# Two feed-forward blocks after an attention: where the split weights lie, how many steps multiply with unsplit weights, and which engine converts and cuts

## The chip, the cores and the metric

One core of one Trainium2 chip runs the whole kernel. The metric is the device time in microseconds (us). TensorE is called PE here, VectorE DVE, ScalarE ACT, GpSimd POOL, and the queue that issues all DMAs SP.

## The reference

An induced attention turns x (12480 x 128) into new tokens by way of 32 inducing points; then two feed-forward blocks follow, each 128 to 2048 to 128:

```python
x = mab(x, mab(I, x))                       # softmax attention, twice
h = x @ moe_w_in;  g = h * clip(h + 3, 0, 6) / 6;   x = g @ moe_w_out
h = x @ moe2_w_in; r = maximum(h, 0);               x = (r * r) @ moe2_w_out
```

The weights arrive as 64-bit floats, and the kernel reads them as 64-bit integers and makes float32 of them itself.

## The kernel before, in words

Tokens lie along the free dimension, in 25 chunks of 512 (one of 192). A chunk takes 8 **steps** of two 128-row feature blocks in each feed-forward block, so that there are K = 200 steps of each. Loop k of the main loop (line 757) runs step k of the first block and step j = k - 11 of the second. The stages of a step are `up1` (L597, two matmuls into `h`), `gate1` (L605 on ACT, L606 on DVE, giving `g`), then `high1` (ACT L615 or POOL L617), which rounds `g` to float32r, `low1` (DVE or POOL, L625), which subtracts that from `g`, and two loops after `up1` the product with w_out, `down1`. In the second block these are `up2` (L674), `relu2` (L685) and `square2` (L689) on ACT, `high2` (ACT L699 or POOL L694), `low2` (DVE L705) and, three loops behind `up2`, `down2`. A split product (`down`, L645, and `up2`) takes three float32r matmuls per feature block: high by high, low weights by high, high by low. In the first N1 = 13 steps of the first block `down_whole` (L633) multiplies the unsplit float32 `g` with the unsplit float32 weights instead; for those steps `high1` and `low1` return at once.

The first weight, w1a (kind "a"), is mixed with the attention's result; the others come in four pieces each of 128 x 512: "b" is moe_w_out, "c" moe2_w_in, "d" moe2_w_out. A piece is loaded as 64-bit words (`load_piece`, L153 or L158), made into float32 by `convert` (DVE L174 masks the sign, POOL L178 clamps, ACT L183 scales the low word, DVE L185 and L189 shift and join, POOL L194 adds), and a b, c or d piece is later split by `cut`: a float32r high part (`wh`, L210 on POOL, L214 on ACT or L216 on DVE) and a low part (`wl`, L218 on DVE or POOL). float32 pieces of kinds b, c and d (`w32`) share 8 rotating buffers, and each high and each low part has a buffer of its own.

What sets the order: `tick()` is called at 26 places before the main loop (16 in the loop over eight groups of tokens, then around the attention's end) and twice in each loop, so that loop k holds ticks 26 + 2k and 27 + 2k. `PLAN` gives for each piece the tick of its conversion, the tick of its cut and the engines of the cut's two instructions. SP runs its DMAs in program order throughout. The other engines run in written order up to the end of the first attention (line 750); from there to loop 23 a scheduler orders each engine's instructions at build time, by written order and by its own model of when each can start; from loop KM = 24 on the written order holds again. In each engine's queue an instruction that waits holds up all behind it.

The attention of chunk c + 1 is spread over loops 8c to 8c + 3: scores on PE (L485), `att_shift` on DVE (L505 to L510), an exponential (L519), `att_norm` (L526 to L534), and `att_spread` (L571 to L581), which sends the result through 16 DMAs of SP (L581) into `a_t`, the right side of `up1` eight steps later. Three PSUM buffers `h` serve `up1`, `up2` and the scores together. At the end of a chunk's `down1`, ACT L662 and DVE L663 read `yacc`, of which there is one, into `yh` and `yl`.

Of the kernel before, what the change touches and what calls it, by code (L numbers as in the profile page):

```python
# [10 lines left out]
F32 = mybir.dt.float32  # L11
F32R = mybir.dt.float32r
# [4 lines left out]
ALU = mybir.AluOpType  # L17
# [20 lines left out]


PLAN = {  # L40
    ("a", 0): (4, None, ""),
    ("a", 1): (6, None, ""),
    ("a", 2): (8, None, ""),
    ("a", 3): (10, None, ""),
    ("b", 0): (13, 58, "sv"),
    ("b", 1): (17, 54, "sv"),
    ("b", 2): (22, 50, "vp"),
    ("b", 3): (29, 55, "vv"),
    ("c", 0): (32, 47, "sp"),
    ("c", 1): (26, 33, "sp"),  # L50
    ("c", 2): (36, 46, "pp"),
    ("c", 3): (50, 57, "sp"),
    ("d", 0): (38, 54, "sp"),
    ("d", 1): (53, 58, "sp"),
    ("d", 2): (53, 62, "pv"),
    ("d", 3): (58, 62, "pv"),
}

HIGH1_S = {0, 1, 3, 4, 6, 7, 9, 13, 14, 18, 19, 20, 22, 23}
LOW1_P = {1, 2, 4, 5, 6, 7, 8, 11}  # L60
HIGH2_P = {0, 1, 6, 7, 10, 12}
LOW2_P = {}
N1 = 13
OFF = 11
L1, L2 = 2, 3
MIX = (0, 3)
PRE = 26
KM = 24
RA, RB = 4, 4
WB = 8  # L70
TAIL = 8
LAST = 2

# [2 lines left out]
def induced_attention_then_two_ffn(  # L76
# [84 lines left out]
    whole, parts, raws, held = {}, {}, {}, []  # L161


    def float_of(item):
        kind, q = item
        if kind == "a":
            return wpool.tile([P, CW], F32, tag=f"hb{q}", name="wa")
        return cv.tile([P, CW], F32, tag="w32", name="w32", bufs=WB)

    def convert(item):  # L170
        words = raws.pop(item)
        low, high = words[:, :, 0], words[:, :, 1]
        e = cv.tile([P, CW], U32, tag="cve", name="cve")
        nc.vector.tensor_scalar(  # L174
            out=e, in0=high, scalar1=0x7FFFFFFF, scalar2=0x7FFFFFFF,
            op0=ALU.bitwise_and, op1=ALU.bitwise_and,
        )
        nc.gpsimd.tensor_scalar(  # L178
            out=e.bitcast(F32), in0=e.bitcast(F32), scalar1=MOST, scalar2=LEAST,
            op0=ALU.min, op1=ALU.max,  # L180
        )
        r = cv.tile([P, CW], I32, tag="cva", name="cva")
        nc.scalar.mul(r, low, 2.0 ** -29)  # L183
        yield
# [12 lines left out]
        while waiting and not todo and sum(i[0] != "a" for i in held) < RB:  # L197
            load_piece(waiting.pop(0))

    def cut(item):  # L200
        kind, q = item
        hi, lo = (
            (wpool if kind == "b" else wpool2).tile([P, CW], F32R, tag=f"{u}{kind}{q}", name=f"w{u}")
            for u in "hl"
        )
        w = whole[item]
        assert ("a", q) not in whole or kind != "b"
        on = [engine_of[i] for i in PLAN[item][2]]
        if on[0] is nc.gpsimd:
            nc.gpsimd.tensor_scalar(  # L210
                out=hi, in0=w, scalar1=1.0, scalar2=1.0, op0=ALU.mult, op1=ALU.mult
            )
        elif on[0] is nc.scalar:
            nc.scalar.copy(hi, w)  # L214
        else:
            nc.vector.tensor_copy(hi, w)  # L216
# [433 lines left out]
    def down1(k):  # L650
# [184 lines left out]
```

## Time and profile before

| | us |
|---|---|
| three runs: median (lowest, highest) | 989.15 (986.91, 991.25) |
| the profiled execution, its own time | 988.34 |
| its span in the trace | 986.5 |
| ACT busy in the span | 816.5 (83%) |
| POOL busy in the span | 274.1 (28%) |

The span is what the profiler sees between the first and the last instruction; 1.8 us of the execution's time lie around it. All rows below are from that one execution.

### The profile page before, as it was taken

The page shows a single profiled execution, that of the slowest core. Times are in us where ns is not written, and L with a number is a line of the kernel's source. Part 1 is how long each engine was busy: PE and PEld are TensorE (multiplying, and loading weights), DVE is VectorE, ACT ScalarE, POOL GpSimd, SP SyncE. Part 2 cuts the span into 40 slices and gives each one's busy share as a digit, 9 for nine tenths or more (in the row PEclk, how much of TensorE's full clock was granted, in tenths as well). Part 3 has the DMA queues.
Part 4 walks back from the last instruction along what each step waited for, and adds up shares of the span by engine and source line. Part 5 has one row for each costly group of instructions (what it writes and reads, how often), then busy time and mean ns, then how long its engine had stood idle before and what let it go on. Part 6 is the DMA issues. An engine that isn't in the chain of part 4 may idle for free.

```text
span 986.5 us, 12958 instructions
## 1 busy us (share of the span) xinstructions
PE 958.1 (97%) x4614; PEld 766.4 (78%) x4614; DVE 810.9 (82%) x980; ACT 816.5 (83%) x928; POOL 274.1 (28%) x417
## 2 busy tenths in 40 slices
PE   8877899999999999999999999999999999999998
PEld 6534678888888888888888888888888888888886
DVE  4788978888888888888887798888888888888864
ACT  6556878888888888888888968888888888888886
POOL 2365312222222222222221232222222222222213
PEclk9897999999999999999999999999999999999999
DMA  9522010110110110100100011001001001000000
GB/s 344 169 71 79 16 33 2 32 32 2 32 33 2 32 33 2 31 26 1 32 26 6 28 33 27 6 27 33 7 27 33 7 27 32 8 15 22 1 11 21
DMA packets 32879, 34.54 MB, mean 35 GB/s; under 512 B 7600, under 2 KB 25008, under 8 KB 32304
## 3 DMA queue, kind: packets, MB, share of 16 engines
q1 hardware_dynamic: 32816, 33.73, 10.9%
q8 instruction: 36, 0.59, 0.3%
q14 instruction: 27, 0.22, 0.1%
HBM read 21.18 MB, written 6.39 MB: 28 GB/s over the span
## 4 chain that ended last, share of the span: by engine, by line
PE 89%; DVE 6%; ACT 2%; DMA 1%; POOL 1%; issue 1%; SPq 0%; DVEq 0%; POOLq 0%
PE oacc L645 26%; PE h L674 26%; PE yacc L645 25%; PE h L597 9%; DVE g L606 1%; DMA raw<-in_w1a 1%; PE ps L485 1%; DVE cve L189 1%; DVE cve L185 1%; DMA xg<-in_xT 1%; PE yacc L633 1%; ACT g L605 1%; PE xt L336 0%; POOL cve L178 0%; POOL wl L218 0%
## 5 line engine op out<-in xcount | busy, mean ns | idle before, releaser
L606 DVE SCALAR_TENSOR_TENSOR g<-g,h 128x1024 f32<-128x1024 f32 (+1 forms) x200 | 238.4, 1193 | 112.9 <-ACT g L605 109.9
L605 ACT ACTIVATE g<-h,three 128x1024 f32<-128x1024 f32 (+1 forms) x200 | 219.1, 1096 | 116.0 <-PE h L597 115.5
L705 DVE TENSOR_TENSOR lo<-g,hi 128x1024 fp32r<-128x1024 f32 (+2 forms) x201 | 241.1, 1200 | 16.4 <-PE oacc L645 10.4
L625 DVE TENSOR_TENSOR lo<-g,hi 128x1024 fp32r<-128x1024 f32 (+1 forms) x187 | 222.3, 1189 | 2.3 <-POOL hi L617 2.3
L689 ACT ACTIVATE g<-g 128x1024 f32<-128x1024 f32 (+2 forms) x201 | 206.6, 1028 | 0.5
L685 ACT ACTIVATE g<-h 128x1024 f32<-128x1024 f32 (+2 forms) x201 | 199.7, 994 | 6.5 <-PE h L674 6.5
L617 POOL TENSOR_SCALAR hi<-g 128x1024 fp32r<-128x1024 f32 (+1 forms) x180 | 185.5, 1030 | 30.5 <-ACT g L685 16.4
L699 ACT CAST hi<-g 128x1024 fp32r<-128x1024 f32 (+2 forms) x188 | 192.1, 1023 | 0.0
L674 PE MATMUL h<-yh,wh 128*128 128x512 f32 (+1 forms) x400 | 154.4, 386 | 2.5 <-ACT g L685 1.5
L674 PE MATMUL h<-yh,wl 128*128 128x512 f32 (+1 forms) x400 | 154.2, 385 | 0.0
L674 PE MATMUL h<-yl,wh 128*128 128x512 f32 (+1 forms) x400 | 153.9, 385 | 0.0
L597 PE MATMUL h<-at,m 128*128 128x512 f32 (+1 forms) x400 | 129.2, 404 | 9.9 <-DVE st L505 5.7
L645 PE MATMUL oacc<-hi,wh 128*128 128x512 f32 (+1 forms) x400 | 122.4, 387 | 0.0
L645 PE MATMUL oacc<-hi,wl 128*128 128x512 f32 (+1 forms) x400 | 121.6, 385 | 0.0
L645 PE MATMUL oacc<-lo,wh 128*128 128x512 f32 (+1 forms) x400 | 121.5, 385 | 0.0
L645 PE MATMUL yacc<-hi,wh 128*128 128x512 f32 (+1 forms) x374 | 114.2, 387 | 3.7 <-DVE yl L663 3.7
L805 POOL COPY turn<-lo 128x1 f32<-128x1 f32 x113 | 21.6, 191 | 337.9 <-DVE lo L625 337.9
L645 PE MATMUL yacc<-lo,wh 128*128 128x512 f32 (+1 forms) x374 | 113.9, 386 | 0.0
L645 PE MATMUL yacc<-hi,wl 128*128 128x512 f32 (+1 forms) x374 | 113.9, 386 | 0.0
L597 PEld LDWEIGHTS h<-at,m 128*128 128x128 f32 x400 | 72.9, 189 | 34.0 <-issue 10.1
L674 PEld LDWEIGHTS h<-yh,wh 128*128 128x128 f32 x400 | 75.3, 188 | 19.1 <-ACT g L685 2.3
L674 PEld LDWEIGHTS h<-yl,wh 128*128 128x128 f32 x400 | 75.2, 188 | 15.3
(118 smaller groups left out, 937.1 us busy)
## 6 DMA issues: line engine op xcount, KB each, us to landing
outT<-osb SPq DMA_DIRECT2D x23, 256.0 KB, 2.2
xc<-in_xT SPq DMA_DIRECT2D x22, 256.0 KB, 2.8
xg<-in_xT SPq DMA_DIRECT2D x4, 1024.0 KB, 7.1
at<-ah SPq DMA_DIRECT2D x184, 16.0 KB, 1.8
at<-al SPq DMA_DIRECT2D x184, 16.0 KB, 1.8
raw<-in_w1a SPq DMA_DIRECT2D x4, 512.0 KB, 8.8
raw<-in_w1b SPq DMA_DIRECT2D x4, 512.0 KB, 8.8
raw<-in_w2a SPq DMA_DIRECT2D x4, 512.0 KB, 4.0
```

The lines of the kernel that those rows point to most:

```text
L597: nc.tensor.matmul(h1[k][:, u, :size[c]], lhsT=m4[:, f * P:(f + 1) * P], rhs=a_t[c], start=True, stop=True)
L605: nc.scalar.activation(g1[k], h, AF.Relu, bias=three)
L606: nc.vector.scalar_tensor_tensor(out=g1[k], in0=g1[k], scalar=6.0, in1=h, op0=ALU.min, op1=ALU.mult)
L617: nc.gpsimd.tensor_scalar(out=hi1[k], in0=g1[k], scalar1=1.0, scalar2=1.0, op0=ALU.mult, op1=ALU.mult)
L625: (nc.gpsimd if k in LOW1_P else nc.vector).tensor_tensor(out=lo1[k], in0=g1.pop(k), in1=hi1[k], op=ALU.subtract)
L645: nc.tensor.matmul(acc, lhsT=w[:, f * P:(f + 1) * P], rhs=g[:, u, :], start=(p == 0 and n == 0), stop=(p == NP - 1 and n == 5),)
L674: nc.tensor.matmul(h2[k][:, u, :size[c]], lhsT=w, rhs=y, start=(n == 0), stop=(n == 2))
L685: nc.scalar.activation(g2[k][:, u, :], h[:, u, :n], AF.Relu)
L689: nc.scalar.activation(g2[k][:, u, :], g2[k][:, u, :], AF.Square)
L699: nc.scalar.copy(hi2[k][:, u, :], g2[k][:, u, :])
L705: (nc.gpsimd if k in LOW2_P else nc.vector).tensor_tensor(out=lo2[k][:, u, :], in0=g[:, u, :], in1=hi2[k][:, u, :], op=ALU.subtract)
L805: nc.gpsimd.tensor_copy(turn[:n], behind_it)
```

## The change

Two constants grow: N1 from 13 to 16 steps with unsplit weights in the first block, and a new N2 = 8 does the same in the second block. Every clamp moves from POOL to DVE, every cut takes ACT for the high and DVE for the low part, and a conversion runs its mask, clamp, scaling, shift and join within one tick. Each float32 b, c and d piece has a buffer of its own, and the low part of a piece is written where the float32 of the piece before it lay (for b0 that of c3; c0 and d0 have an extra buffer each). Raw buffers of b, c and d grow from 4 to 7. The ticks of nearly all conversions and cuts change. The last lines of `down2` use the chunk's size for 512, which is the last chunk's size too.

```diff
+    ("a", 0): (4, None), ("a", 1): (6, None), ("a", 2): (8, None), ("a", 3): (10, None),
-    ("b", 0): (13, 58, "sv"),
-    ("b", 1): (17, 54, "sv"),
-    ("b", 2): (22, 50, "vp"),
-    ("b", 3): (29, 55, "vv"),
-    ("c", 0): (32, 47, "sp"),
-    ("c", 1): (26, 33, "sp"),
-    ("c", 2): (36, 46, "pp"),
-    ("c", 3): (50, 57, "sp"),
-    ("d", 0): (38, 54, "sp"),
-    ("d", 1): (53, 58, "sp"),
-    ("d", 2): (53, 62, "pv"),
-    ("d", 3): (58, 62, "pv"),
+    ("b", 0): (13, 53), ("b", 1): (17, 57), ("b", 2): (22, 61), ("b", 3): (26, 65),
+    ("c", 0): (33, 36), ("c", 1): (37, 40), ("c", 2): (41, 44), ("c", 3): (45, 49),
+    ("d", 0): (48, 62), ("d", 1): (52, 66), ("d", 2): (56, 70), ("d", 3): (60, 74),
...
-HIGH1_S = {0, 1, 3, 4, 6, 7, 9, 13, 14, 18, 19, 20, 22, 23}
-LOW1_P = {1, 2, 4, 5, 6, 7, 8, 11}
-HIGH2_P = {0, 1, 6, 7, 10, 12}
-N1 = 13
+HIGH1_S = {18, 19, 20, 22, 23}
+HIGH2_P = {10, 12}
+N1, N2 = 16, 8
-RA, RB = 4, 4
-WB = 8
+RA, RB = 4, 7
...
     def float_of(item):
...
-        return cv.tile([P, CW], F32, tag="w32", name="w32", bufs=WB)
+        return (wpool if kind == "b" else wpool2).tile([P, CW], F32, tag=f"w{kind}{q}", name="w32")
+
+    def lower_of(item):
+        kind, q = item
+        pool, tag = (wpool if kind == "b" else wpool2), f"w{kind}{q - 1}"
+        if q == 0:
+            pool, tag = wpool2, {"b": "wc3", "c": "lc", "d": "ld"}[kind]
+        return pool.tile([P, CW], F32R, tag=tag, name="wl")
...
     def convert(item):
...
-        nc.gpsimd.tensor_scalar(
+        nc.vector.tensor_scalar(
             out=e.bitcast(F32), in0=e.bitcast(F32), scalar1=MOST, scalar2=LEAST,
             op0=ALU.min, op1=ALU.max,
         )
         r = cv.tile([P, CW], I32, tag="cva", name="cva")
         nc.scalar.mul(r, low, 2.0 ** -29)
-        yield
         nc.vector.tensor_scalar(
...
     def cut(item):
...
-        w = whole[item]
+        w = whole.pop(item)
...
+        nc.scalar.copy(hi, w)
         yield
-        on[1].tensor_tensor(out=lo, in0=w, in1=hi, op=ALU.subtract)
+        lo = lower_of(item)
+        nc.vector.tensor_tensor(out=lo, in0=w, in1=hi, op=ALU.subtract)
...
     def high2(k):
+        if k < N2:
+            return
...
     def low2(k):
+        if k < N2:
+            return
...
     def down2(k):
...
+        if k < N2:
+            down_whole(oacc[c], g2.pop(k), "d", p)
+        else:
+            down(oacc[c], hi2.pop(k), lo2.pop(k), "d", p, by_side=k == K - 1)
```

## Rows read from the trace of the kernel before

**Rows 1.** The page's busy time and share of the span by engine.

```profile
PE 958.1 (97%) x4614; PEld 766.4 (78%) x4614; DVE 810.9 (82%) x980; ACT 816.5 (83%) x928; POOL 274.1 (28%) x417
PEclk9897999999999999999999999999999999999999
```

**Rows 2.** Windows: stretch, length, busy PE, PEld, DVE, ACT, POOL, granted clock, DMA.

```profile
45.00:72.00 27.00, 21.52 (x60) 9.35 (x60) 22.94 (x40) 16.06 (x23) 16.05 (x16) 1.00 0.24 68
72.00:85.00 13.00, 5.74 (x19) 2.51 (x19) 12.93 (x18) 6.06 (x9) 7.09 (x6) 0.67 0.45 144
85.00:128.60 43.60, 38.29 (x144) 26.64 (x143) 37.37 (x46) 32.68 (x35) 18.00 (x16) 0.94 0.05 13
128.60:300.00 171.40, 171.40 (x779) 140.37 (x778) 144.90 (x160) 148.80 (x157) 41.70 (x67) 1.00 0.08 24
```

**Rows 3.** Chain in order of time: start, us, what; one whole step, two split ones.

```profile
50.08 1.72 PE yacc L633 x4
...
129.22 1.36 PE h L674 x6
...
133.76 1.36 PE h L674 x6
```

**Rows 4.** PE's timeline at loops 0, 8, 10 and 19, and one wait.

```profile
45.10 0.74 PE L597 MATMUL h<-at,m 128*128 128x512 f32 x2 [0.68 <-DVE cve L174]
...
73.75 0.70 PE L597 MATMUL h<-at,m 128*128 128x512 f32 x2 [1.90 <-DMA at<-al]
...
80.02 1.22 PE L597 MATMUL h<-at,m 128*128 128x512 f32 x2 [4.55 <-DVE st L505]
...
124.20 1.19 PE L645 MATMUL yacc<-hi,wh 128*128 128x512 f32 x2 [2.79 <-DVE yl L663]
...
128.61 0.62 PE L597 MATMUL h<-at,m 128*128 128x512 f32 x2
```

**Rows 5.** Timelines of DVE, POOL and ACT between loops 8 and 10.

```profile
71.31 1.48 DVE L216 CAST wh<-w 128x512 fp32r<-128x512 f32 x1
73.72 1.51 DVE L185 TENSOR_SCALAR cve<-cve 128x512 uint32<-128x512 uint32 x1
...
73.23 3.13 POOL L218 TENSOR_TENSOR wl<-w,wh 128x512 fp32r<-128x512 f32 x2
...
78.62 0.62 ACT L214 CAST wh<-w 128x512 fp32r<-128x512 f32 x1 [4.97 <-POOL w L194]
```

**Rows 6.** Groups by line and shape, 45 to 125 us: busy, mean ns | idle before.

```profile
L705 DVE TENSOR_TENSOR lo<-g,hi 128x1024 fp32r<-128x1024 f32 x5 | 6.9, 1381 | 0.5 <-ACT hi L699 0.5
L625 DVE TENSOR_TENSOR lo<-g,hi 128x1024 fp32r<-128x1024 f32 x5 | 6.0, 1209 | 0.0
L185 DVE TENSOR_SCALAR cve<-cve 128x512 uint32<-128x512 uint32 x10 | 7.3, 734 | 4.3 <-POOL cve L178 4.3
L178 POOL TENSOR_SCALAR cve<-cve 128x512 f32<-128x512 f32 x10 | 7.2, 726 | 9.1 <-DVE cve L174 4.8 <-DVE le L528 4.2
L699 ACT CAST hi<-g 128x1024 fp32r<-128x1024 f32 x4 | 4.2, 1047 | 0.0
L214 ACT CAST wh<-w 128x512 fp32r<-128x512 f32 x7 | 4.4, 622 | 8.4 <-POOL w L194 8.4
```

**Rows 7.** One line's instructions over the whole span: ns min/median/max, first and last start.

```profile
L185 DVE TENSOR_SCALAR cve<-cve x16: 416/427/1524, 14.7 to 99.2; 128x512 uint32<-128x512 uint32 x16
L218 DVE TENSOR_TENSOR wl<-w,wh x5: 677/1092/1754, 72.7 to 104.0; 128x512 fp32r<-128x512 f32 x5
```

**Rows 8.** SP's timeline: the first spread's 16 DMAs.

```profile
62.35 5.03 SPq L581 DMA_DIRECT2D at<-ah  x8
67.48 4.96 SPq L581 DMA_DIRECT2D at<-al  x8
```

**Rows 9.** DVE's timeline around b1's conversion, tick 17.

```profile
38.56 0.29 DVE L440 TENSOR_TENSOR ht<-ph,rec 128x128 f32<-128x128 f32 x1 [0.74 <-PE ph L439]
...
39.22 0.69 DVE L189 SCALAR_TENSOR_TENSOR cve<-raw,cve 128x512 uint32<-128x512 uint32 x1
```

More of the change, by code (lines that the diff above doesn't have):

```diff
@@ L40 @@
 PLAN = {
[L41 to L44, printed above, removed]
-    ("b", 0): (13, 58, "sv"),
-    ("b", 1): (17, 54, "sv"),
-    ("b", 2): (22, 50, "vp"),
-    ("b", 3): (29, 55, "vv"),
-    ("c", 0): (32, 47, "sp"),
-    ("c", 1): (26, 33, "sp"),
-    ("c", 2): (36, 46, "pp"),
-    ("c", 3): (50, 57, "sp"),
-    ("d", 0): (38, 54, "sp"),
-    ("d", 1): (53, 58, "sp"),
-    ("d", 2): (53, 62, "pv"),
-    ("d", 3): (58, 62, "pv"),
-}
-HIGH1_S = {0, 1, 3, 4, 6, 7, 9, 13, 14, 18, 19, 20, 22, 23}
-LOW1_P = {1, 2, 4, 5, 6, 7, 8, 11}
-HIGH2_P = {0, 1, 6, 7, 10, 12}
-LOW2_P = {}
-N1 = 13
+    ("a", 0): (4, None),
+    ("a", 1): (6, None),
+    ("a", 2): (8, None),
+    ("a", 3): (10, None),
+    ("b", 0): (13, 53),
+    ("b", 1): (17, 57),
+    ("b", 2): (22, 61),
+    ("b", 3): (26, 65),
+    ("c", 0): (33, 36),
+    ("c", 1): (37, 40),
+    ("c", 2): (41, 44),
+    ("c", 3): (45, 49),
+    ("d", 0): (48, 62),
+    ("d", 1): (52, 66),
+    ("d", 2): (56, 70),
+    ("d", 3): (60, 74),
+}
+HIGH1_S = {18, 19, 20, 22, 23}
+HIGH2_P = {10, 12}
+N1, N2 = 16, 8
 OFF = 11
@@ L139, in induced_attention_then_two_ffn @@
     LEAST, MOST = (struct.unpack("f", struct.pack("I", n))[0] for n in (0x38000000, 0x47EFFFFF))
-    engine_of = {"v": nc.vector, "p": nc.gpsimd, "s": nc.scalar}
     src_of = {"a": w1a, "b": w1b, "c": w2a, "d": w2b}
@@ L201, in cut @@
         kind, q = item
[L202 to L205, printed above, removed]
-        w = whole[item]
-        assert ("a", q) not in whole or kind != "b"
[L208 to L216, printed above, removed]
+        hi = (wpool if kind == "b" else wpool2).tile([P, CW], F32R, tag=f"h{kind}{q}", name="wh")
+        w = whole.pop(item)
+        assert ("a", q) not in whole or kind != "b"
+        nc.scalar.copy(hi, w)
         yield
-        on[1].tensor_tensor(out=lo, in0=w, in1=hi, op=ALU.subtract)
+        lo = lower_of(item)
+        nc.vector.tensor_tensor(out=lo, in0=w, in1=hi, op=ALU.subtract)
         parts[item] = hi, lo
@@ L233, in tick @@
                 live.remove(g)
-        for item, (when, cut_at, _) in PLAN.items():
+        for item, (when, cut_at) in PLAN.items():
             if when == n:
@@ L238, in tick @@
                 next(live[-1])
-        for item, (when, cut_at, _) in PLAN.items():
+        for item, (when, cut_at) in PLAN.items():
             if cut_at == n:
@@ L624, in low1, with down_whole @@
         lo1[k] = ep.tile([P, 2, size[k // NP]], F32R, tag="lo1", name="lo1")
-        (nc.gpsimd if k in LOW1_P else nc.vector).tensor_tensor(
+        nc.vector.tensor_tensor(
             out=lo1[k], in0=g1.pop(k), in1=hi1[k], op=ALU.subtract
         )
-    def down_whole(acc, g, p):
-        w = whole["b", p // 2]
+    def down_whole(acc, g, kind, p):
+        w = whole[kind, p // 2]
         for u in range(2):
@@ L654, in down1 @@
         if k < N1:
-            down_whole(yacc[c], g1.pop(k), p)
+            down_whole(yacc[c], g1.pop(k), "b", p)
         else:
@@ L704, in low2 @@
         for u in sides(k):
-            (nc.gpsimd if k in LOW2_P else nc.vector).tensor_tensor(
+            nc.vector.tensor_tensor(
                 out=lo2[k][:, u, :], in0=g[:, u, :], in1=hi2[k][:, u, :], op=ALU.subtract
@@ L712, in down2 @@
             oacc[c] = ap_.tile([P, size[c]], F32, tag="o", name="oacc")
-        down(oacc[c], hi2.pop(k), lo2.pop(k), "d", p, by_side=k == K - 1)
+        if k < N2:
+            down_whole(oacc[c], g2.pop(k), "d", p)
+        else:
+            down(oacc[c], hi2.pop(k), lo2.pop(k), "d", p, by_side=k == K - 1)
         if p == NP - 1:
@@ L721, in down2 @@
             for i, copy in enumerate((nc.vector.tensor_copy, nc.scalar.copy)):
-                half = slice(i * CH // 2, (i + 1) * CH // 2)
+                half = slice(i * size[c] // 2, (i + 1) * size[c] // 2)
                 copy(o[:, half], acc[:, half])
-                nc.sync.dma_start(outT[:, n:n + CH][:, half], o[:, half])
+                nc.sync.dma_start(outT[:, n:n + size[c]][:, half], o[:, half])
     def on(f, k):
```

## The prediction

> **What bounds the kernel now.** I read the page first: PE is busy 97% of the span, DVE 82%, POOL 28% [rows 1]. A kernel with such a share can gain only where PE works less or where the missing part lies. The windows show where that is [rows 2]: from 128.6 us on PE is busy for the whole of every stretch at full clock. Before that, from the first `up1` at 45.10 us [rows 4], come 83.5 us of ramp with PE at 21.5 of 27, 5.7 of 13 and 38.3 of 43.6 us, at a granted clock as low as 0.67 in the middle one, between the levels of 1.2 and 2.4 GHz. In these three stretches DVE is busy 22.9, 12.9 and 37.4 us, 73.2 of 83.6. So two limits meet: DVE with its weight work in the ramp, PE afterwards.
>
> PE's prices come from the chain. Six split matmuls take 1.36 us, a step of two unsplit products 1.72, and a steady step of both blocks 133.76 - 129.22 = 4.54 us [rows 3], which is 3 x 1.36 and 0.45 for `up1`. The marks of loops 0, 8 and 19 are at 45.10, 73.75 and 128.61 us [rows 4]; loop 11 starts at 85.0. What PE needs in each stretch, full and without a wait:
> - A, 45 to 72 us: 8 `up1` (3.6), 8 unsplit products (13.8), some 2 for the mixing and the scores: 19.5 of 27.
> - B, 72 to 85 us: 3 `up1`, one unsplit product, the scores: 3.5 of 13.
> - C, 85 to 128.6 us: 8 `up1` (3.6), 4 unsplit (6.9), 4 split in the first block, 8 `up2` and 5 `down2` (17 x 1.36 = 23.1), 0.8 for scores: 34.4 of 43.6.
>
> The ramp therefore holds 26 us in which PE waits or runs slowly, and that is the most that there is to win. PE's own waits name DVE: 4.55 us before loop 10 for L505, 2.79 us at the turn of a chunk for `yl` [rows 4]. In B one sees why: DVE is full, with `wh` casts and `wl` subtractions of cuts that are written for loops 12 to 16 and were ordered early, and ACT sits 4.97 us in front of a cut's high part that waits for POOL's add, with `gate1` behind it [rows 5].
>
> **The change part by part.** The profiled execution, 988.3 us, lies 0.8 under the median of 989.15; the sum goes from it and is moved by 0.8 at the end.
>
> *More unsplit steps.* Eleven steps go from 1.36 to 1.72 us on PE: +0.36 each, 4.0 in all. Steps 13 to 15 of the first block and 0 to 4 of the second lie in C, which then needs 34.4 + 2.9 = 37.3 us of PE. Steps 5 to 7 of the second, in loops 19 to 21, lie where PE is full: **+1.1 us** straight on the end. In return DVE loses `low1` three times (1.21) and `low2` eight times, six of them in C (1.38): 3.6 + 8.3 = 11.9 us of its 37.4 there [rows 6]. ACT loses six roundings of 1.05 us, POOL five.
>
> *Cuts.* Seven low parts come to DVE, five high parts to ACT (0.62 each [rows 6]), and two DVE casts go. A low part on DVE took 0.68 us undisturbed and 1.75 at worst [rows 7]. I take 0.69, since POOL keeps only its adds in the ramp, against clamps, high and low parts before. The low parts of b can no longer come early: they wait for a buffer, c3's or the piece's before, which PE or another cut still reads. B so loses two casts of 1.48 [rows 5] and three low parts, at the median 1.09 [rows 7]: 6.2 us of DVE. By written order eight cuts fall up to loop 18; the last four (b3, d1 to d3) fall where DVE is busy 144.9 of 171.4 and ACT 148.8 [rows 2]; 0.7 and 0.6 us are free there per step against 0.69 and 0.62 in every second loop, so they cost nothing. Without that cover it would be at most 1.2 us.
>
> *Clamps.* POOL's clamp (0.73 mean) goes, and with it DVE's waits for it, 4.3 us over ten conversions [rows 6]. DVE gets ten clamps. None on DVE is in the trace; the nearest row is the shift L185, of the same shape and kind, 0.43 undisturbed, 1.52 at worst [rows 7]. At 0.43 the ten cost 4.3, as much as the waits that go. The gain is in what stays: L185 itself has a mean of 0.73, 0.31 over its undisturbed time [rows 6, 7], 3.1 over ten, and half of that, 1.5, I count in A.
>
> What the rows show of disturbance: the 1.51 us shift at 73.72 ran beside POOL's `wl` of 73.23 [rows 5]. The Trainium skill (SBUF — State Buffer, Who interferes with whom) says that a DVE instruction such as a scalar operation or one with two SBUF inputs and a POOL instruction exclude each other for the whole length of the one that came first. By that rule the change puts both its clamps and its low parts on the side that can be shut out by POOL's adds, and the sum would go by the worst values, as in the last rival; the trace agrees as far as the two durations of L185 go.
>
> *Conversions in one tick.* In the ordered part before the main loop, b1's shift and join ran after `ht`; now clamp, shift and join, 0.43 + 0.43 + 0.69 [rows 7, 9], stand before it, where DVE had 0.74 us of idle [rows 9]: **+0.8 us** on the way to the first `up1`. The bounds are 0 and 1.6.
>
> *Loads and buffers.* With seven raw buffers SP issues c's pieces and d0 to d2 ahead of the first spread. They wait for conversions up to tick 26, loop 0, and the spread is in loop 3, so nothing; if such a load did hold SP, loop 8 would be late by the same time, for the 16 DMAs of the spread take SP from 62.35 to 72.44 [rows 8] and PE waited 1.90 us for the last [rows 4]. The new wait of a low part for its buffer would hold DVE's `gate1` behind it; but b0 was last read whole in loop 11 and b1's low part is written in loop 16, d0's last whole product is in loop 15 and its buffer is written in loop 20. Four loops of some 4.5 us lie between. Nothing, then. The last lines of `down2` change nothing.
>
> *The sum by stretches.* Before A +0.8. A: -1.5 (bounds +5, all six clamps of A at worst and no relief, and -3). B: DVE's 12.9 of 13 lose 6.2 and get two clamps; 13 - 6.2 + 0.9 = 7.7, and I take **-5** (bounds 0 and -8). C: DVE goes to 37.4 - 11.9 and gets three clamps, one more conversion of 2 us and four more low parts: 31.6, below PE's 37.3. PE becomes the limit; I leave 1.8 us of waits, the turn of a chunk first: 39.1, **-4.5** (bounds -2 and -6.3, PE's floor). Later +1.1. In all 0.8 - 1.5 - 5 - 4.5 + 1.1 = -9.1: 988.3 - 9.1 + 0.8 = **980 us**. Late next are the spread's DMAs before loop 8, then PE.
>
> **The rivals.**
> - *PE already limits from loop 8.* B shrinks to 3.5 and the 1.9 us wait for the spread, C to 37.3, A by 3: 0.8 - 3 - 7.6 - 6.3 + 1.1 = -15, 974 us. For it: in B and C DVE's bill falls below PE's. Against it: a step passes PE, ACT, DVE and PE one after another, and loops 8 to 10 have few steps in flight.
> - *The spread keeps loop 8 where it is, and B fills again.* With seven raw buffers the scheduler can order c's and d's conversions (2 us of DVE each) early into B as it did with the cuts. Then A and B keep their length: 0.8 - 4.5 + 1.1 = -2.6, 986.5 us. For it: ten microseconds of DMA issue that nothing shortens [rows 8], and a queue in which early weight work held ACT for 4.97 us [rows 5]. Against it: fewer instructions are there to be ordered early, and ACT need not wait for POOL's clamps.
> - *DVE limits the ramp more than before.* Place: stretches A and B, where DVE had 4.1 us free. If clamps meet POOL's adds, ten at 1.52 cost 15.2 instead of the 4.3 of waits that go, 11 more, and A, where six are, grows by 5; B gains nothing and C only 2: 0.8 + 5 - 2 + 1.1 = +4.9, 994 us. It decides when the mean clamp passes some 1 us. Against it: conversions are at least three ticks apart, so that an add seldom meets the next clamp.
> - *The unsplit form gives nothing back,* since DVE's freed time in C is not on the path: then only its cost stays, +4.0, less B's 5: about the same time as before. It is a part of the second case's weight.
>
> **How the numbers follow.** A measurement of this kernel can tell about 0.5%, 4.9 us, from no change: faster is below 984.2, slower above 994.1. I give the forecast 0.46, PE from loop 8 on 0.18, the refilled B (with the fourth) 0.22, DVE the limit 0.14. Faster: 0.43 of the forecast, 0.18, and 0.03 of the third = 0.64; slower: 0.10 of the last; the same: 0.26. Faster and same hold most of it. The range runs from 971, a little below the first rival, to 992, short of the last: some 0.05 and 0.12 are left out. The forecast's own range is 976 to 985.
>
> **What would show it.** Right: loop 11 starts near 79 us and loop 19 near 120; from there steps of 4.54 us, three of them 0.36 longer; the clamp on DVE near 0.45 us in the mean; no wait of ACT for POOL's add before `gate1` in B; low parts of b only from loop 13 on; DVE below 33 us in C with PE nearly full. Wrong: a mean clamp above 1 us; loop 11 still at 85 with DVE full in B; PE waiting in C for anything but the turn of a chunk; a wait of DVE for PE in front of a low part; gaps in PE in loops 18 to 24, where d's cuts were held to be covered.

## The result, and the profile after

The changed kernel takes 978.09 us (median of five runs, 977.28 to 981.75) against 989.15. The ratio on record, from all runs of both, is 0.9906 [0.9882, 0.9931], that of the two medians alone 0.9888: faster by about 1%. The forecast was 980. The profiled execution took 978.09 us too, with a span of 976.3, 10.2 below the span of before. The page of the changed kernel, to set beside [rows 1]:

```profile
PE 958.8 (98%) x4592; PEld 761.6 (78%) x4592; DVE 798.7 (82%) x990; ACT 814.7 (83%) x927; POOL 245.2 (25%) x386
...
PEclk9799999999999999999999999999999999999999
```

PE does 0.7 us more and ends 10.2 us earlier; POOL lost 29 us, DVE 12. Where the time went is read from the starts of `up1` on PE's timeline of the changed kernel (beside [rows 4]): loops 0, 8, 11, 19, 20 and 23, and between them the scores and the mixing ahead of loop 0.

```profile
39.75 0.65 PE L478 MATMUL ps<-xlast,ht 128*32 128x128 f32 x8 [1.20 <-DVE ht L433]
...
41.17 3.75 PE L455 MATMUL mixed<-wa,ht 128*128 128x512 f32 x4
...
47.10 0.74 PE L590 MATMUL h<-at,m 128*128 128x512 f32 x2 [0.67 <-DVE cve L178]
...
74.20 0.70 PE L590 MATMUL h<-at,m 128*128 128x512 f32 x2 [3.15 <-DMA at<-al]
...
78.81 1.03 PE L590 MATMUL h<-at,m 128*128 128x512 f32 x2
...
116.46 1.03 PE L590 MATMUL h<-at,m 128*128 128x512 f32 x2
...
121.40 1.03 PE L590 MATMUL h<-at,m 128*128 128x512 f32 x2
...
136.26 0.62 PE L590 MATMUL h<-at,m 128*128 128x512 f32 x2
```

A step of both blocks takes 4.94 us from loop 19 to loop 20 (121.40 - 116.46), which is 4.54 and 0.40 for the second block's unsplit product (0.36 in the prediction). Before, loop 23 started at 146.74. The table goes by loops; the prediction cut A from B at 72 us, 1.75 us ahead of loop 8, and C at loop 19. So, in us:

| stretch | before | after | difference | predicted |
|---|---|---|---|---|
| up to loop 0 | 45.10 | 47.10 | +2.0 | +0.8 |
| A, loops 0 to 8 | 28.65 | 27.10 | -1.55 | -1.5 |
| B, loops 8 to 11 | 11.25 | 4.61 | -6.64 | -5 |
| C and later, loops 11 to 23 | 61.74 | 57.45 | -4.29 | -4.5 + 1.1 |
| loop 23 to the end | 839.8 | 840.0 | +0.3 | 0 |

The windows of the changed kernel (columns as in [rows 2]), one for three microseconds of the way to loop 0, then A, B, C and what follows:

```profile
39.00:42.00 3.00, 2.25 (x12) 1.17 (x13) 1.28 (x4) 0.27 (x2) 1.26 (x1) 0.50 0.54 182
...
47.00:74.20 27.20, 21.99 (x60) 10.51 (x61) 24.95 (x47) 17.97 (x27) 6.74 (x5) 0.94 0.16 49
74.20:78.80 4.60, 3.63 (x18) 1.72 (x19) 4.60 (x9) 4.33 (x6) 1.61 (x1) 1.00 0.47 168
78.80:116.40 37.60, 37.47 (x127) 22.23 (x126) 29.38 (x52) 29.76 (x35) 8.52 (x6) 1.00 0.08 20
116.40:300.00 183.60, 183.42 (x824) 147.23 (x823) 152.34 (x169) 158.40 (x168) 43.50 (x71) 1.00 0.07 21
```

From loop 11 to 19 PE is full (37.47 of 37.6 us) and DVE is down to 29.38 of 37.6 us, where 37.37 of 43.6 stood. In A DVE is fuller than before and PE waits 3.15 us for the last DMA of the spread. B's three steps take 4.6 us.

The groups of weight work in the changed kernel, 45 to 125 us (columns as in [rows 6]): low parts, high parts, shift, clamp.

```profile
L211 DVE TENSOR_TENSOR wl<-w,wh 128x512 fp32r<-128x512 f32 x11 | 7.5, 682 | 1.2 <-ACT wh L208 0.7 <-PE oacc L626 0.6
...
L208 ACT CAST wh<-w 128x512 fp32r<-128x512 f32 x12 | 7.3, 618 | 6.7 <-POOL w L197 6.6
...
L188 DVE TENSOR_SCALAR cve<-cve 128x512 uint32<-128x512 uint32 x10 | 5.0, 512 | 0.0
...
L182 DVE TENSOR_SCALAR cve<-cve 128x512 f32<-128x512 f32 x10 | 4.3, 439 | 0.0
```

Single lines over the span (as [rows 7]: ns min/median/max, first and last start), clamp and low part:

```profile
L182 DVE TENSOR_SCALAR cve<-cve x16: 412/420/636, 13.9 to 91.6; 128x512 f32<-128x512 f32 x16
...
L211 DVE TENSOR_TENSOR wl<-w,wh x12: 673/680/693, 62.6 to 146.8; 128x512 fp32r<-128x512 f32 x12
```

The low part, 1.09 us in the median and 1.75 at worst before [rows 7], now takes 0.68 each time. The clamp's mean is 0.44. The wait of ACT for POOL's add is still there, 6.6 us in all against 8.4 [rows 6], but by ACT's timeline 4.7 us of it lie ahead of loop 8, where PE waits for the spread. The longest wait of all, and the `gate1` of loop 8, which it didn't hold up:

```profile
72.98 0.62 ACT L208 CAST wh<-w 128x512 fp32r<-128x512 f32 x1 [2.90 <-POOL w L197]
...
74.94 3.15 ACT L598 ACTIVATE g<-h,three 128x1024 f32<-128x1024 f32 x3 [0.28 <-PE h L590]
```

### The profile page after: what moved, and what is told of

Its sections match the earlier page's. It is cut to its first block, busy times and chain, and to the rows that moved or that the text cites. A ratio compares the mean times of both kernels' runs of the same rounds, so it can differ in the third digit from the quotient of the medians.

```text
span 976.3 us, 12891 instructions
## 1 busy us (share of the span) xinstructions
PE 958.8 (98%) x4592; PEld 761.6 (78%) x4592; DVE 798.7 (82%) x990; ACT 814.7 (83%) x927; POOL 245.2 (25%) x386
## 4 chain that ended last, share of the span: by engine, by line
PE 89%; DVE 4%; ACT 1%; issue 0%; SPq 0%; DMA 0%; POOL 0%; DVEq 0%; ACTq 0%; POOLq 0%
PE h L667 26%; PE oacc L638 26%; PE yacc L638 25%; PE h L590 9%; DVE g L599 1%; PE oacc L626 1%; PE ps L478 1%; PE yacc L626 1%; DVE lo L702 0%; SPq L574 0%; DVE lo L618 0%; ACT g L598 0%; DVE wl L211 0%; DVE cve L192 0%; DVE yl L656 0%
## 5 line engine op out<-in xcount | busy, mean ns | idle before, releaser
L702 DVE TENSOR_TENSOR lo<-g,hi 128x1024 fp32r<-128x1024 f32 (+2 forms) x193 | 230.3, 1194 | 12.6 <-PE oacc L638 7.2
L618 DVE TENSOR_TENSOR lo<-g,hi 128x1024 fp32r<-128x1024 f32 (+1 forms) x184 | 219.5, 1193 | 9.0 <-ACT hi L608 5.6
L694 ACT CAST hi<-g 128x1024 fp32r<-128x1024 f32 (+2 forms) x184 | 187.8, 1021 | 0.0
L590 PE MATMUL h<-at,m 128*128 128x512 f32 (+1 forms) x400 | 132.8, 414 | 5.7 <-DMA at<-al 3.2
L638 PE MATMUL oacc<-hi,wl 128*128 128x512 f32 (+1 forms) x384 | 116.7, 385 | 0.0
L638 PE MATMUL oacc<-hi,wh 128*128 128x512 f32 (+1 forms) x384 | 116.6, 385 | 0.0
L638 PE MATMUL oacc<-lo,wh 128*128 128x512 f32 (+1 forms) x384 | 116.6, 384 | 0.0
L638 PE MATMUL yacc<-hi,wh 128*128 128x512 f32 (+1 forms) x368 | 111.8, 385 | 1.1 <-DVE yl L656 1.1
L638 PE MATMUL yacc<-lo,wh 128*128 128x512 f32 (+1 forms) x368 | 111.6, 385 | 0.0
L638 PE MATMUL yacc<-hi,wl 128*128 128x512 f32 (+1 forms) x368 | 111.6, 384 | 0.0
```

Of the source, the lines that this page charges most:

```text
L590: nc.tensor.matmul(h1[k][:, u, :size[c]], lhsT=m4[:, f * P:(f + 1) * P], rhs=a_t[c], start=True, stop=True)
L618: nc.vector.tensor_tensor(out=lo1[k], in0=g1.pop(k), in1=hi1[k], op=ALU.subtract)
L638: nc.tensor.matmul(acc, lhsT=w[:, f * P:(f + 1) * P], rhs=g[:, u, :], start=(p == 0 and n == 0), stop=(p == NP - 1 and n == 5),)
L702: nc.vector.tensor_tensor(out=lo2[k][:, u, :], in0=g[:, u, :], in1=hi2[k][:, u, :], op=ALU.subtract)
```

## The experiments

All runs with their stretches as in the table above, in us. Each was timed against the kernel before on its own chip, in three rounds (the last one in five); that kernel's own median was 988.11, 987.22 and 986.95 us on the three chips of these runs, so that medians of different rows can differ by a microsecond for the chip alone. Span and stretches come from one profiled execution each. A mark that follows an unsplit product can stand up to 0.43 us early, since its record begins while PE still works.

| run | loop 0 | 0 to 8 | 8 to 11 | 11 to 23 | span | median | ratio |
|---|---|---|---|---|---|---|---|
| before | 45.1 | 28.7 | 11.25 | 61.7 | 986.5 | 989.15 | |
| after | 47.1 | 27.1 | 4.6 | 57.5 | 976.3 | 978.09 | 0.9906 [0.9882, 0.9931] |
| before_new_engines | 43.8 | 28.9 | 4.6 | 61.0 | 977.6 | 979.83 | 0.9918 [0.9901, 0.9935] |
| cuts_as_before | 47.4 | 26.5 | 9.7 | 58.5 | 982.1 | 982.53 | 0.9936 [0.9914, 0.9957] |
| b_lows_own_buffers | 47.3 | 27.1 | 6.6 | 58.5 | 979.6 | 981.08 | 0.9931 [0.9915, 0.9947] |
| raw5 | 47.2 | 27.0 | 4.7 | 57.5 | 976.1 | 978.50 | 0.9914 [0.9899, 0.9929] |
| no_unsplit_added | 47.5 | 27.0 | 6.1 | 58.3 | 978.9 | 978.76 | 0.9916 [0.9902, 0.9930] |
| n2_zero | 48.3 | 27.1 | 4.6 | 59.5 | 979.4 | 980.23 | 0.9915 [0.9897, 0.9933] |
| n1_13 | 46.4 | 27.4 | 5.3 | 56.9 | 976.1 | 976.95 | 0.9883 [0.9866, 0.9900] |
| clamps_on_pool | 43.7 | 25.2 | 7.5 | 58.0 | 974.0 | 976.19 | 0.9875 [0.9850, 0.9901] |
| two_ticks | 44.0 | 25.6 | 6.5 | 58.3 | 974.5 | 976.61 | 0.9894 [0.9881, 0.9907] |
| b1_tick_18 | 46.5 | 27.0 | 4.6 | 57.5 | 975.9 | 977.38 | 0.9889 [0.9869, 0.9908] |
| spread_earlier | 46.6 | 26.6 | 4.8 | 58.1 | 976.1 | 977.81 | 0.9901 [0.9879, 0.9923] |
| two_ticks_n1_13 | 44.5 | 26.5 | 6.5 | 62.0 | 979.6 | 980.97 | 0.9927 [0.9909, 0.9945] |

**Who gave B its 6.6 us: engines or buffers?** First the engines alone, put into the kernel before; ticks, steps and buffers stay as they were. (The edit also gives two tile pools another name; with the old names the program comes out the same, instruction for instruction.)

```diff
-        nc.gpsimd.tensor_scalar(
+        nc.vector.tensor_scalar(
             out=e.bitcast(F32), in0=e.bitcast(F32), scalar1=MOST, scalar2=LEAST,
...
-    ("b", 2): (22, 50, "vp"),
+    ("b", 2): (22, 50, "sv"),
...
```

> The kernel before, with clamps on DVE and every cut with its high part on ACT and its low part on DVE; ticks, buffers, steps as before. Theory (engines make a part of the gain in loops 8 to 11, cuts that come early the rest): loops 0 to 8 as before within 1.5 us, loops 8 to 11 at 7 to 9 us in place of 11.25, loops 11 to 23 as before, since DVE still has all subtractions: 985.5 us, 983 to 988. Rival A (engines are everything in loops 8 to 11): 4.6 us there, 982.5. Rival B (DVE as a fuller queue makes it worse without the unsplit steps): 990 or above.

This part alone brings 979.8 us, and B is 4.6 us, as short as after the whole change. PE's timeline at loops 8 and 11 of that kernel:

```profile
72.70 0.70 PE L597 MATMUL h<-at,m 128*128 128x512 f32 x2 [0.80 <-DMA at<-al]
...
77.28 1.03 PE L597 MATMUL h<-at,m 128*128 128x512 f32 x2
```

And its DVE timeline, with three low parts ahead of loop 8:

```profile
69.50 2.36 DVE L218 TENSOR_TENSOR wl<-w,wh 128x512 fp32r<-128x512 f32 x2
...
72.12 0.68 DVE L218 TENSOR_TENSOR wl<-w,wh 128x512 fp32r<-128x512 f32 x1
```

By the order of the built program these are the low parts of c2, c0 and b2; one of the first two took 1.76 us, yet they lie ahead of loop 8, and B loses nothing by them. The low parts of b1, b3 and b0, which before started at 72.7, 77.8 and 79.1, come here at 88.0, 96.5 and 101.5, all behind loop 11, though no buffer keeps them back: the scheduler's order changed with the engines. DVE's timelines of the kernel before (b3 and b0) and of this run (b1):

```profile
77.77 1.96 DVE L218 TENSOR_TENSOR wl<-w,wh 128x512 fp32r<-128x512 f32 x2
...
88.02 1.76 DVE L218 TENSOR_TENSOR wl<-w,wh 128x512 fp32r<-128x512 f32 x1
```

Then the other way round: the changed kernel with each cut on the two engines that it had before.

```diff
-        nc.scalar.copy(hi, w)
+        on = CUT_ON[item]      # sv sv vp vv  sp sp pp sp  sp sp pv pv
+        if on[0] == "p":
+            nc.gpsimd.tensor_scalar(
...
-        nc.vector.tensor_tensor(out=lo, in0=w, in1=hi, op=ALU.subtract)
+        (nc.gpsimd if on[1] == "p" else nc.vector).tensor_tensor(
+            out=lo, in0=w, in1=hi, op=ALU.subtract
+        )
```

> The kernel after, with each cut's high and low part on the engines that the kernel before gives them (seven low parts and three high parts on POOL, two high parts on DVE); ticks, buffers, clamps and steps as after. Theory (POOL's cuts shut DVE out and, queued with POOL's adds, hold up conversions): the shift, clamp and join on DVE show maxima of 1.4 us and more again, loops 0 to 11 take 3 to 5 us longer, loop 11 to 23 at most 1 longer: 982 us, 980 to 984. Rival (the gain came from where low parts lie and from the ticks, which keep b's cuts out of loops 8 to 11; the engines don't matter): within 1.5 us of after, 977 to 980.

B is 9.7 us again, 5.1 of the 6.6, and the median 4.4 us higher, though the shared buffers stay and no low part of b comes ahead of loop 11 (the first, b0's, at 84.2). The DVE timeline of this run has the casts and a disturbed mask:

```profile
71.25 1.48 DVE L220 CAST wh<-w 128x512 fp32r<-128x512 f32 x1
...
73.66 1.50 DVE L182 TENSOR_SCALAR cve<-raw 128x512 uint32<-128x512 uint32 x1
75.08 1.49 DVE L220 CAST wh<-w 128x512 fp32r<-128x512 f32 x1
```

Its ACT timeline has the high part that waits, with `gate1` of loop 8 behind it, at 77.41:

```profile
76.32 0.62 ACT L218 CAST wh<-w 128x512 fp32r<-128x512 f32 x1 [2.69 <-POOL w L201]
```

The third run gives b's low parts buffers of their own, so that they can come early; to make room the raw buffers go from 7 to 5, and raw5 does that alone.

```diff
-RA, RB = 4, 7
+RA, RB = 4, 5
...
-        if q == 0:
+        if kind == "b":
+            tag = f"lb{q}"
+        elif q == 0:
```

> The kernel after, with buffers of their own for b's four low parts (so that they may be cut early) and 5 raw buffers instead of 7, which makes room for them; nothing else. Theory (what shortened loops 8 to 11 is that b's low parts cannot come early any more): two to four of L211's instructions on b move into loops 4 to 11, 0.7 us each on DVE, and loops 8 to 11 grow by 1 to 3 us from 4.6: 979 to 980 us. Rival (the engines of the cuts, without casts on DVE and without POOL, did it, and four early low parts of 0.7 us do no harm): within 1 us of after, 977 to 979.

> The kernel after, with 5 raw buffers instead of 7; nothing else. It is the other half of the run with buffers of their own for b's low parts. Theory (early low parts of b cost the 3 us of that run): within 1 us of after, 977 to 979, loops 8 to 11 near 4.6. Rival (fewer raw buffers, so later loads and conversions, cost them): 980.5 or above, loops 8 to 11 near 6.6.

Against raw5 this costs 3.5 us of the span, 1.9 of it in B, and 2.6 in the medians (the ranges, 980.6 to 981.4 and 977.7 to 980.75, just touch). By the order of the built program only one low part of b came early, b0's, ahead of loop 8; it was disturbed, by b_lows_own_buffers' DVE timeline:

```profile
72.00 1.75 DVE L213 TENSOR_TENSOR wl<-w,wh 128x512 fp32r<-128x512 f32 x1
```

So the engines are enough for B, and those of the cuts are needed. The shared buffers are not what won it. Two raw buffers fewer cost nothing that shows.

**How much of B is waiting, and how much the clock.** Windows from loop 8 to loop 11 (columns as in [rows 2]) of before, before_new_engines, cuts_as_before, b_lows_own_buffers, two_ticks (a run shown further down) and no_unsplit_added (the next one); the changed kernel's is the line of 74.20:78.80 above.

```profile
73.75:85.00 11.25, 5.74 (x19) 2.48 (x19) 11.18 (x17) 4.94 (x7) 5.43 (x4) 0.62 0.51 163
...
72.70:77.28 4.58, 3.65 (x18) 1.72 (x19) 4.36 (x10) 3.71 (x4) 0.00 (x0) 1.00 0.97 307
...
73.83:83.53 9.70, 5.73 (x18) 2.46 (x19) 9.70 (x14) 5.57 (x8) 5.90 (x5) 0.64 0.25 80
...
74.40:80.98 6.58, 5.69 (x18) 2.42 (x19) 6.58 (x12) 5.15 (x7) 1.29 (x1) 0.64 0.87 279
...
69.55:76.03 6.48, 5.54 (x18) 2.25 (x19) 6.48 (x13) 5.57 (x9) 1.27 (x1) 0.67 0.40 119
...
74.55:80.67 6.12, 6.12 (x19) 3.03 (x19) 5.13 (x9) 4.73 (x7) 1.59 (x1) 0.53 0.39 127
```

The length less the busy PE is idle time: 5.51 us before, 0.97 after. So 4.54 of B's 6.64 us are waits of PE that went, the 4.55 us for DVE [rows 4] above all. The other 2.11 are the clock: about the same matmuls took 5.74 and 3.63 us, with 0.62 and 1.00 granted, that is, before, a part of the stretch at the lower level. before_new_engines has neither loss (0.93 us idle, clock 1.00), cuts_as_before has both. b_lows_own_buffers and two_ticks have PE idle no longer than the changed kernel (0.89 and 0.94 us): what their B is longer by is PE at the lower clock, beside a DVE that is full with one more conversion; the two weren't told apart. That the clock alone can do it is seen in no_unsplit_added. Up to loop 11 its instructions and their order on each engine are those of the changed kernel; its B takes 6.1 us and not 4.6, and PE isn't idle in it at all. Why the clock fell in one of these two executions and not in the other is not known. A difference of 1.5 us in B between two single executions thus need not come from the edit.

**What do the unsplit steps give in C?** The changed kernel without the added ones (the split ones need their cuts earlier), then with one half of them each (n2_zero takes of the diff what concerns d, n1_13 what concerns b).

```diff
-N1, N2 = 16, 8
+N1, N2 = 13, 0        # n2_zero: 16, 0    n1_13: 13, 8
-HIGH1_S = {18, 19, 20, 22, 23}
+HIGH1_S = {13, 14, 18, 19, 20, 22, 23}
-HIGH2_P = {10, 12}
+HIGH2_P = {0, 1, 6, 7, 10, 12}
-    ("b", 0): (13, 53), ("b", 1): (17, 57), ("b", 2): (22, 61), ("b", 3): (26, 65),
+    ("b", 0): (13, 52), ("b", 1): (17, 54), ("b", 2): (22, 56), ("b", 3): (26, 58),
-    ("d", 0): (48, 62), ("d", 1): (52, 66), ("d", 2): (56, 70), ("d", 3): (60, 74),
+    ("d", 0): (48, 51), ("d", 1): (52, 55), ("d", 2): (56, 59), ("d", 3): (60, 63),
```

> The kernel after with both step counts as before (N1 = 13, N2 = 0, roundings on the engines of before), b's cuts at ticks 52 to 58 and d's three ticks after their conversions; engines, ticks of conversions and buffers of after. Theory (the unsplit steps win what the two single runs show, +2.1 for the second block's and about -1 for the first's, and PE needs 4.0 us less): loop 11 to 23 takes 59 to 60.5 us against 57.5 of after; 979.5 us, 978 to 981.5. Rival (both kinds together keep DVE off the path and neither alone shows it): loop 11 to 23 at 61 or more, as in the kernel before with new engines, 982.

> The kernel after, with the second block split from its first step (N2 = 0, the four highs of steps 0, 1, 6 and 7 on POOL as before) and d's pieces cut three ticks after their conversion, since the split parts are then needed from loop 14 on. Theory (DVE and ACT, not PE, set loops 11 to 19 when all steps round and subtract): PE needs 8 x 0.36 = 2.9 us less, but DVE gets 8 x 1.2 us of subtractions back; from loop 11 to loop 23 the 57.5 us of after become 59 to 62, DVE full and PE with gaps: 981 us, 979 to 984. Rival (DVE's time there is not on the path; unsplit steps only cost PE time): 2.9 us shorter, 975.

> The kernel after, with 13 unsplit steps in the first block as before (highs of steps 13 and 14 on ACT) and b's cuts at ticks 52, 54, 56 and 58, which is as late as the split steps 13 to 15 allow in order. Theory: PE 1.1 us less in loops 15 to 17, DVE 3.6 us and ACT 2.1 us more in loops 13 to 16, where DVE of after has some 8 us of 37.6 free and ACT as much; the relief is then not needed for these three steps, and the time is between 977 and 980, nearer 978. Rival (the three steps are needed to keep DVE off the path): from loop 11 to 23 more than 2 us longer, 980 or above.

Windows from 78 to 140 us (busy PE is the first number after the length, DVE the third). The changed kernel:

```profile
78.00:140.00 62.00, 61.87 (x221) 39.76 (x220) 46.85 (x67) 51.24 (x57) 10.57 (x8) 1.00 0.08 22
```

Without the added unsplit steps:

```profile
78.00:140.00 62.00, 59.16 (x232) 43.35 (x232) 59.88 (x78) 54.71 (x61) 19.99 (x13) 0.95 0.05 13
```

DVE went down by 13 us and PE became full, as forecast, but the stretch from loop 11 to 23 is only 0.8 us shorter by it (58.3 and 57.5), and a part of that can be the clock (0.95 and 1.00). For what fills PE is in the main the 4.0 us that the unsplit products take by the prediction's price. The medians differ by 0.7 us and their intervals overlap. The halves differ: by the four medians the second block's eight steps win 2.1 or 1.8 us (980.23 to 978.09, 978.76 to 976.95) and the first block's three lose 1.1 or 1.5, on chips whose own medians differ by up to 1.2. Without the second block's eight steps the turn of a chunk comes back on PE's timeline, at n2_zero's first product of the next chunk, and 11 to 23 is 2.0 longer:

```profile
116.97 0.70 PE L638 MATMUL yacc<-hi,wh 128*128 128x512 f32 x2 [3.27 <-DVE yl L656]
```

Without the first block's three, 11 to 23 is 0.6 *shorter*, near to the 1.1 us of PE that goes; in the medians that is 1.1 us, within what the runs scatter.

The rest of C's gain is in before_new_engines against no_unsplit_added: 61.0 and 58.3, with the same unsplit steps and engines, but other ticks, buffers and conversions in one tick. The waits of PE in the former (us in all, times, longest), 78 to 140 us, name d's low parts, which that plan cuts in ticks 54 to 62:

```profile
PE oacc L645 <- DVE wl L218: 3.1, 3, 1.8
```

**Clamp and tick.** Two runs put the tick back that stood between scaling and shift; one also puts the clamp back on POOL.

```diff
-        nc.vector.tensor_scalar(
+        nc.gpsimd.tensor_scalar(                     # clamps_on_pool alone
             out=e.bitcast(F32), in0=e.bitcast(F32), scalar1=MOST, scalar2=LEAST,
...
         nc.scalar.mul(r, low, 2.0 ** -29)
+        yield                                        # clamps_on_pool and two_ticks
         nc.vector.tensor_scalar(
```

> The kernel after, with the clamp of each conversion back on POOL and the shift and join one tick later, as before; cuts, steps, buffers and ticks as after. Theory (clamps on DVE cost what DVE's waits for POOL's clamps cost, and the join ahead of `ht` is what made loop 0 late): loop 0 returns from 47.1 to about 45.1 us, loops 0 to 8 take 1 to 2 us more than the 27.1 of after because POOL again shuts DVE out, loops 8 to 11 some 1 us more, loop 11 on unchanged: 978 us, 976 to 980. Rival (the clamps on POOL were the main thing that held the ramp): loops 8 to 11 grow back by 4 us or more and the time is 982 or above.

> The kernel after, with the conversion over two ticks as before (mask, clamp and scaling in the first, shift and join in the second), the clamp staying on DVE; nothing else. Theory (the time that the run with clamps on POOL won over after came from the two ticks, which take two DVE instructions from in front of `ht`, and not from POOL): loop 0 at 43.5 to 45 us in place of 47.1, loops 8 to 11 at 4.6 as in after, loop 11 to 23 unchanged: 975 us, 974 to 976.5. Rival (it came from POOL's clamps): time as after, 978.

They end within 0.4 us of each other: which engine clamps is worth nothing that shows. Both start loop 0 some 3 us earlier than the changed kernel, and loop 8 by 5.4 and 4.6, to 68.8 and 69.6. But loops 8 to 11 take 7.5 and 6.5 in place of 4.6, and 11 to 23 0.5 and 0.8 more, so that some 2 us of the span are left. From loop 0 to 8 these kernels do one conversion less (5 joins, not 6); it comes in B instead, where the clock is also lower (0.67 in two_ticks, above).

**Two ways to win loop 0 and loop 8 alone.** b1's conversion one tick later, and the first spread one step earlier.

```diff
-    ("b", 1): (17, 57),
+    ("b", 1): (18, 57),                              # b1_tick_18
...
-            if p == 2:
+            if p == (1 if c == 0 else 2):            # spread_earlier: att_norm
-            if p == 3:
+            if p == (2 if c == 0 else 3):            # spread_earlier: att_spread
```

> The kernel after, with b1's conversion at tick 18 in place of 17, so that its four DVE instructions stand behind `ht` and not ahead of it; nothing else. Theory (the join ahead of `ht` put off `ht` by 0.85 us, PE idled 1.2 us in front of the scores and ran the stretch after it at half clock): `ht` at 38.5 us, loop 0 at 45 to 45.5 in place of 47.1, and all marks after it earlier by 1.5 to 2: 976.3 us. Rival (loop 0 is not what sets loop 8, since the spread's DMAs do): loop 0 earlier, loop 8 still at 74.2, time as after, 978.

> The kernel after, with chunk 1's attention one loop shorter: its normalisation in loop 1 and its spread in loop 2 instead of 2 and 3; nothing else. Theory (with DVE relieved, loop 8 waits for the last of the 16 DMAs, 3.15 us of idle PE): the spread's first DMA leaves 2 to 3 us earlier than 62.7, loop 8 starts 2 to 3 us earlier than 74.2, and the later marks follow: 975.5 us, 974.5 to 977. Rival (conversions that fill the wait of PE on DVE are the limit, so they only move behind loop 8): loop 8 earlier, but loop 11 still near 78.8 and the time as after.

With b1 later the wait for `ht` is 0.38 us again, as before, but the mixing still runs at 0.50 of the clock, and loop 0 is only 0.6 us earlier. PE's timeline of b1_tick_18:

```profile
39.07 0.66 PE L478 MATMUL ps<-xlast,ht 128*32 128x128 f32 x8 [0.38 <-DVE ht L433]
...
40.50 3.75 PE L455 MATMUL mixed<-wa,ht 128*128 128x512 f32 x4
```

And one of its windows, with the clock behind POOL's number:

```profile
39.00:42.00 3.00, 2.93 (x13) 1.51 (x14) 2.49 (x8) 0.57 (x2) 0.86 (x1) 0.50 0.50 194
```

The same four products took 2.91 us before, 2.85 in two_ticks and 1.89 in clamps_on_pool. PE's timeline before, and in clamps_on_pool:

```profile
40.34 2.91 PE L462 MATMUL mixed<-wa,ht 128*128 128x512 f32 x4
...
38.83 1.89 PE L456 MATMUL mixed<-wa,ht 128*128 128x512 f32 x4
```

The spread's first DMA came at 61.80 in spread_earlier, where the changed kernel's SP timeline has 62.73; loop 8 moved by 0.9 to 73.3, of which 0.5 are loop 0's, and B and C gave it back.

**Both small gains together:** two_ticks with N1 = 13.

```diff
+        yield                                        # as in two_ticks
-N1, N2 = 16, 8
+N1, N2 = 13, 8                                       # and the rest of n1_13
```

> The kernel after with two changes that each looked like a gain: the conversion over two ticks, and 13 unsplit steps in the first block (b's cuts at ticks 52 to 58, highs of steps 13 and 14 on ACT). Theory: loop 0 some 2 to 3 us earlier, loop 11 to 23 some 0.5 us shorter, PE 1.1 us less; the two add: 974 us, 972.5 to 975.5. Rival (loops 0 and 8 are decoupled by the spread, or the two-tick conversions delay DVE where steps 13 to 15 need it): 977.

They don't add: 980.97 us, where each alone had 976.6 and 976.95. (Its six executions lie from 976.89 to 982.40, wider apart than those of any other run; the profiled one took 981.38.) Loops 11 to 23 grew to 62.0, and PE's waits (40 to 140 us) have the turn of a chunk again:

```profile
PE yacc L639 <- DVE yl L657: 2.0, 1, 2.0
```

No version tried is clearly faster than the changed kernel: the intervals of clamps_on_pool and two_ticks, the lowest medians, overlap its own.

## Why the prediction was right, and where its steps were not

**The sum** was right, 980 for 978.1, and so was the picture: DVE limits the ramp, PE what follows; what can be won lies between loops 0 and 19. That it came so near is in part luck: 1.2 us too little on the way to loop 0 stood against 1.6 too little gain in B and 0.9 in C, and the causes that were charged with B and C are not the ones that the runs show. Nothing after loop 23 moved (+0.3), and from 116.4 to 300 us PE is busy 183.42 of 183.60, so the late cuts (b3, d1 to d3) are covered as forecast. Of the signs, loop 11 came at 78.81 (79 forecast), loop 19 at 116.46 ("near 120"; the prediction's own terms add up to 118.4), and low parts of b come from loop 13 on. One sign of being wrong came once, without harm: DVE waited 0.55 us for PE in front of a low part, at 101.06.

**Up to loop 0: +2.0, not +0.8.** The step named, `ht` behind b1's conversion, cost what was forecast. On the changed kernel's DVE timeline clamp, shift and join stand ahead of `ht`, which starts at 39.41, not 38.56 [rows 9]:

```profile
37.88 0.43 DVE L182 TENSOR_SCALAR cve<-cve 128x512 f32<-128x512 f32 x1
38.34 0.43 DVE L188 TENSOR_SCALAR cve<-cve 128x512 uint32<-128x512 uint32 x1
38.80 0.69 DVE L192 SCALAR_TENSOR_TENSOR cve<-raw,cve 128x512 uint32<-128x512 uint32 x1
39.41 0.28 DVE L433 TENSOR_TENSOR ht<-ph,rec 128x128 f32<-128x128 f32 x1
...
71.87 1.37 DVE L188 TENSOR_SCALAR cve<-cve 128x512 uint32<-128x512 uint32 x1
```

What was left out is the clock. Both kernels run at the lower level from about 35 us on, but before it rose within the mixing, and after only behind it. Two windows of before, then one of after, beside that of 39 to 42 us above:

```profile
39.00:42.00 3.00, 3.00 (x13) 1.42 (x14) 1.91 (x6) 0.57 (x2) 1.26 (x1) 0.50 0.28 75
42.00:45.00 3.00, 2.32 (x11) 1.26 (x9) 2.81 (x8) 1.91 (x5) 0.00 (x0) 0.95 0.25 102
...
42.00:45.00 3.00, 3.00 (x6) 1.19 (x5) 2.33 (x8) 1.13 (x4) 0.00 (x0) 0.50 0.48 174
```

So the mixing took 3.75 us, not 2.91, and the fills behind it 0.97, not 0.60. That is the other 1.2 us.

**A: -1.55, forecast -1.5, but the reason is not shown.** The shift did lose its disturbance (0.51 in the mean for 0.73, 2.2 us over ten). But clamps_on_pool, with POOL's clamps, has an A of 25.2, shorter still with one conversion less in it. What bounds A's end is the spread, for which PE waits 3.15 us.

**B: -6.6, forecast -5; the attribution failed.** The step "The low parts of b can no longer come early: they wait for a buffer" charged a half of the gain to the buffers. The casts and b's low parts did leave B, as it says, but they leave it as well in before_new_engines, where each low part has a buffer of its own: the engines alone give all of it. The casts were in the way (cuts_as_before, 9.7, with no low part of b in B). Whether an early low part costs anything by itself stays open (b_lows_own_buffers: one came early, and the longer B is PE at the lower clock). What the step left out is that clock, 2.11 of the 6.64 us; the prediction read the 0.67 in B but put no price on it.

**C and later: -4.3, forecast -3.4; the attribution failed here too.** DVE fell below PE and PE filled up, as forecast, but the 11.9 us of DVE that unsplit steps free were not worth C's 4.5. By the chain before, before_new_engines, no_unsplit_added, after (61.7, 61.0, 58.3, 57.5) the engines gave 0.7, the ticks, buffers and conversions in one tick 2.7, the unsplit steps 0.8, the last with the clock at 0.95 and 1.00. That is close to the fourth rival, which I held for a small part of a case: their price on PE eats what DVE gives back. What the price buys is the second block's half, the turn of a chunk. In the spans the eleven steps seem worth 2.6 us, but 1.5 of that lie in B and 0.4 ahead of loop 0, where both kernels run the same instructions; that leaves what C has, 0.8, near to the 0.7 of the medians.

**Clamps: even, as forecast.** At 0.44 us in the mean and 0.64 at worst, far below the 1 us from which the last rival decides. That one engine shuts the other out is still seen: the shift of 1.37 us above began while POOL's add (71.64, 1.31 us) ran. By the Trainium skill (SBUF — State Buffer, Who interferes with whom) the clamps and the low parts can be hit so. The traces agree in kind: a clamp of two_ticks took 1.37 us (at 68.0, while an add of POOL ran), four low parts of before_new_engines 1.53 to 1.76. But of the changed kernel's 16 clamps none took over 0.64 and of its low parts none over 0.69. An add comes after the join, and by then the next clamp or low part seems seldom due there.

**The rivals.** "PE limits from loop 8" is what the trace looks like from loop 8 on, with a B of 4.6 us; its 974 failed on A (1.5 us), the way to loop 0 (1.2), and about 1 us each in B and C. "B fills again" is not what the change did; in clamps_on_pool and two_ticks an earlier loop 8 was paid back in B, by a conversion that came there and by the lower clock.

## What to carry to other kernels

When several parts of a change free the same engine in the same stretch, each looks like the cause and their savings are not additive: run the cheapest part alone in the old kernel before the costly one is credited. Here eleven lines of engine choices gave 8.9 of 10.2 us of the span (7.4 us in the medians on that run's chip), and the unsplit products, which fill PE, won 0.7 or 0.8 us beyond what they cost. A busy share that rises to full says that a limit is reached, not that time was won. And before a difference of a microsecond or two in one stretch is put down to an edit, set PE's idle time and the granted clock of that stretch side by side.

## What was not expected of the hardware

The clock ahead of loop 0 differed between kernels whose instructions there are the same or nearly so: 0.50 in the window of 39 to 42 us in the changed kernel and in b1_tick_18, 0.66 in two_ticks, 1.00 in before_new_engines and clamps_on_pool, and four matmuls cost 3.75, 2.85 or 1.89 us by it. In the changed kernel PE had stood idle for 1.12 us at 31.7 us, behind b0's conversion in one tick. That alone doesn't sort them: it was 0.52 in two_ticks, before_new_engines and clamps_on_pool, but also in the kernel before, which had 0.50 in that window. Among the kernels with that conversion in one tick loop 0 starts anywhere from 46.4 to 48.3 us, and n2_zero, the latest, has the same instructions up to there as the changed kernel with 47.1, so that a difference of 1 us in the span of two of them need not come from the edit.
